# Early v loads issued from GpSimd's queue, and a new order of steps, in an attention and wave-mixing kernel

## The chip, the cores and the metric

The kernel runs on one core of a Trainium2 chip. A core has a matmul engine (TensorE, PE in the profile; its weight loads are PEld), a vector engine (VectorE, DVE), an activation engine (ScalarE, ACT), GpSimd (POOL) and SyncE (SP), which here only issues DMAs. Each engine works through its own queue in order and waits on semaphores for the others. Sixteen DMA engines move the data of all queues. The metric is the device time of one execution in microseconds; lower is better.

## The reference

Inputs are q, k and v of shape 8 batches x 8 heads x 576 positions x 64, and four weights. Everything is float32 outside the kernel; the kernel computes on bfloat16 tiles with float32 sums.

```python
q_d, k_d, v_d = (t.reshape(B, H, S // 4, 4, D).mean(axis=3) for t in (q, k, v))
out_up = np.repeat(sm_attn(q_d, k_d, v_d), 4, axis=2)       # pooled attention, repeated
mask = np.abs(pos[:, None] - pos[None, :]) < 4
out_local = softmax(where(mask, q @ k.T / 8, -1e9)) @ v     # a band of 7 positions
x = (out_up + out_local) with heads joined: (B, 576, 512)
theta = x @ w_theta
y = einsum(w_tok_r, x * cos(theta)) + einsum(w_tok_i, x * sin(theta))   # over positions
u = x + y
return u + maximum(u @ w_ch, 0)
```

## The kernel before, in words

A batch goes through these stages. Its inputs come in 13 loads into staging tiles `st` (15 buffers used in rotation, shared with the weights' loads): four k chunks and four q chunks of two heads each (288 KB), and five v chunks `v0` to `v4` of two windows of 64 positions each. A v chunk is loaded as two halves of 128 KB, one per window, with all eight heads; the half's rows are 64 positions x 8 heads of 256 bytes, so 512 runs. All loads are issued by SP (L220 for v, L223 for k and q, L253 and L255 for weights). Each chunk is then cast to bfloat16 (step C) on DVE, ACT or POOL.

PE turns k and q (A, L300), a copy takes the result out of PSUM (a), DVE and POOL form the sums of four positions (d, L317; e, L334 and L335 on POOL). The local attention has scores, exp, mask, outputs and their scaling (S, s, m, O, o, i). The pooled attention first sums v over four positions with a matmul against pooling matrices `pu` (U: L348 for the chunks 0 to 3, L350 for chunk 4), copies that out (u), spreads the last part with two products on POOL (x, L363), then has scores, exp, output and scaling (P, p, N, n). Both are joined in `xT` (T, t). Theta, its cosine and sine and the products with x follow (H, h, X, y), then the mix over positions (J, L654, against `WT`, which PE builds early from the token weights by the steps V and v), the sum with x (j, L663), the channel product (K, L693) and the last step with its store (b, D).

Constants (step k) are built on POOL: the identity `ident`, the `band`, three pooling matrices `pu`, and `own`; some fills are on DVE.

The order of all of this is written out by hand as one long string, `ORDER` (L66): each letter is the next step of its sequence, and the order of the letters is the order of the instructions on every engine's queue. `BANKS` (L81) gives the PSUM bank of each step that needs one, in that order, and `ENGINES` (L87) says for the steps C, a, c, f, q, u and v which engine does each copy (v DVE, a ACT, p POOL).

Of the kernel before, what the change touches and what calls it, by code (L numbers as in the profile page):

```python
# [26 lines left out]
W = 64  # L27
# [11 lines left out]

BY_QUEUE = [6, 7]  # L40

OC = 96


@with_exitstack
def kernel(
# [11 lines left out]
    nc = tc.nc  # L58
# [5 lines left out]


    ORDER = (  # L66
        "kLCLkLkCk2ACLCkaAkLCkLLCLLLCdlCaAAaaSkLkklSLLedSLLePsLCmsCOOmLkLsPpCCLlCookipULOuuxxLoCCOCNiioCCcN1l"
        "nLinTAAnnQcaClcaATLCmqtacCtOAHdTaoiSlhLXLdtyTeleLLsSPtsHPlCCmOpcLpSCsmloCTiOCcUlOtocuXuHoiOhcCiVhxom"
        "xNyiCGccHLALLganLVvVnLZVvLzNVlvVlXClvvLCnVnyCAQlvValhCACCveVLqXcvTtTcaAvlTtyaOoticHdTS2STsLsdecJHcJV"
        "LhcXttJvVhyVCVCvvvlXVyvLGVCVLVLgJLvZCvLVvvPjjjpCmJUjLuuHOxjoCiCOPJpxomiLNCXnHjLJnChNjAcLCJnyhCnLXjyT"  # L70
        "azCQLAAJCqaAlTLlLdJtLaSaLCjtOsoOiceJjjoCSLmLCJcTiClOtjsLCSCUHCRJeCuoiTTudRsCxLLjACtLJhaLtALJaGjmgOOj"
        "xPoJRoCiHiCcSpPjedCCXRKsLpmbyhKNZACnXbLHyaCLHhnXKyCLNhLLAbXzfKLCamUnSnyCuLfOJojCLiQRuCJJbAdsCLjJTmqR"
        "SjaOtjJCoseTAixxCatPPjpRLKdRDALLKJbCpSmbCOasToiNLtADnJLLjCnaNLLOnSHoiTLCjCJLnTtsOLjhotRCOCCLHXTiQohG"
        "HygDXiHThLmqhLCXZytztAKyTCabHODhLOteoLUumHDoiuiXRKhyRCfOCSbSJTsRoiLJsLdjCxADajtJejLPOpPLmopJxTDdtXjN"
        "JnnyDRjGJXCgNjHJmhniACHnaCCKjZLyLLCCbXQAChTdqRCKXyabKJySb2sLUjuKOzeutLSoesmCbCLCLSiJTmDJDjsCOPCjRpPo"
        "iJRLpOtjOoOoixHLioxTCChJiNAatnDJCHjDRndNALTLhKTtHnabnCtXeKQOjJyCoRbjGiTXgKhLHqKAFmhfLRZbJXbajyXAzJCy"
        "TyjtOaSJsoTiDtECjOromSUJuetTiKSRDsDstdOHjJJbHuxojTjJmthRiDPOYMOjhxJpJofiOomjiMOFjPoJpNiMjRNDnHnnofTn"
        "KKQbDhiGqEKTKbMtgHZRbyrzTKRhDTtYTyytbyHttKHDFJEGJhMjgbHjJDHhJMMjJrJZbMhDjyyjJzhDjRjyJjyKJJRJRKJYbJjD"
        "RKJjRjbjfRbJjDJjKjKjKKKfDREKbbRKDDbFDbbbrDDDYbD"
    )  # L80
    BANKS = (  # L81
        "0246024602467406240652064102456042605201650216452014601246012540160254602367012045106450164067340626"
        "4502610542612046025045620154062706420654205672065476025764205645074206742074620634062047016420176451"
        "0462107426107642076425062450215420346534203675204670246230463046230461346023026743126317430143064132"
        "604524360467253640234602043201450346751047236054176370101054231067542350167"
    )
    ENGINES = dict(  # L87
        C=(
            "vapaaaaavpvvappppppapppvpapppppppppppppvapvpappvappapppppppavpvapappaapppaaaaapppppaaaapapppappp"
            "appaavaa"  # L90
        ),
        a="avaavaaaavaaaaaaaaaaaaaaaaaaaaaa",
        c="aapapppappppppppappp",
        f="ppvpapap",
        q="vaaavvva",
        u="vavvavavaaaaaaaa",
        v="vvvvaaaavvvvaavaaa",
    )


# [25 lines left out]
    def copy(step, **operands):  # L126
        copies[next(engines[step])](**operands)  # L127
# [79 lines left out]
    def stage(key):  # L207
        t = staged[key] = rot("st", [P, S], FP32, 15)
        return t
# [3 lines left out]
    def load(b):  # L213
        for it in ITEMS:
            c = int(it[1])
            if it[0] == "v":
                t = stage((b, it))[:, 0:DM].rearrange("p (h d) -> p h d", d=D)
                for g in range(2):
                    lo = W0[2 * c + g]
                    nc.sync.dma_start(out=t[W * g:W * g + W], in_=v[b, :, lo:lo + W, :].rearrange("h p d -> p h d"))  # L220
            else:
                src = k if it[0] == "k" else q
                nc.sync.dma_start(out=stage((b, it)), in_=src[b, 2 * c:2 * c + 2].rearrange("h (p r) d -> (h p) (r d)", r=WR))  # L223
            yield
# [24 lines left out]
    def weight_loads():  # L249
        for kind, i, ct in WITEMS:  # L250
            t = stage((kind, i, ct))
            if kind == "tok":
                nc.sync.dma_start(out=t[0:OC], in_=(moe_w_tok_r, moe_w_tok_i)[i][OC * ct:OC * ct + OC, :])  # L253
            else:
# [3 lines left out]
    def weight_casts():  # L258
        for kind, i, ct in WITEMS:
            t = staged.pop((kind, i, ct))  # L260
            if kind == "tok":
                copy("c", out=w_tm[i][0:OC, ct, :], in_=t[0:OC])
            else:
# [5 lines left out]
    def weight_turns():  # L269
        for hf in range(2):  # L270
            for j in range(9):
                ps = held["w", hf, j] = one(BF16)
                for ct in range(3):
                    for ri in ((j % 2,) if j < 8 else (0, 1)):
                        lo, n = (0, P) if j < 8 else (HALF * ri, HALF)
                        nc.tensor.transpose(
                            out=ps[lo:lo + n, OC * ct:OC * ct + OC],
                            in_=w_tm[ri][0:OC, 3 * hf + ct, P * (j // 2):P * (j // 2) + n],
                            identity=ident[0:OC, 0:OC],
                        )  # L280
# [462 lines left out]
    def each(steps, n=B):  # L743
# [3 lines left out]
    sequences = {  # L747
        "k": constants(), "1": table(AF.Sin), "2": table(AF.Exp),
        "L": each(load), "C": each(cast), "l": weight_loads(), "c": weight_casts(), "V": weight_turns(), "v": weight_turns_out(),
        "A": each(turns), "a": each(turns_out), "d": each(key_sums), "e": each(query_sums),  # L750
        "U": each(pooled_v), "u": each(pooled_v_out), "x": each(pooled_v_last),
# [49 lines left out]
```

## Time and profile before

| | us |
|---|---|
| median of 3 runs | 246.65 |
| lowest, highest | 245.88, 248.42 |
| the profiled execution | 245.89 |
| its span, first to last instruction | 244.2 |
| mean granted TensorE clock | 0.979 |

The next lines are the page's list of DMA issues: what is loaded or stored, the engine that issues it, how many, the size of each, and the median time from issue to landing.

```profile
st<-in_v_dram SPq DMA_DIRECT2D x80, 128.0 KB, 5.1
st<-in_k_dram SPq DMA_DIRECT2D x32, 288.0 KB, 4.8
st<-in_q_dram SPq DMA_DIRECT2D x32, 288.0 KB, 5.3
out_dram<-osb SPq DMA_DIRECT2D x31, 256.0 KB, 3.3
```

All times are those of one execution. A row of a group gives the line, the engine, the operation, the tiles written and read with their shapes, the count, then busy time and the mean of one, and last the idle time of the engine just before them with what ended it. In the 40 slices each digit is the busy share of a slice in tenths. The chain is the work that ended last, followed back from the last instruction.

### The profile page before, as it was taken

To read this page: it belongs to the slowest core of one execution; us is meant where nothing else is said; L and a number is where in the kernel's file an instruction comes from. 1 tells how busy PE (TensorE), PEld (TensorE's weight loads), DVE (VectorE), ACT (ScalarE), POOL (GpSimd) and SP (SyncE) were. 2 spreads that over 40 slices of the span, in tenths; PEclk is the share of its full clock that TensorE was granted. 3 is DMA by queue.
4 is the path that set the end of the run, shared out by engine and by line. 5 is a ranking of instruction groups with operands and counts; after the bars stand their busy time and mean duration, and the time that the engine had idled before them with its cause. 6 is when DMAs were issued, how large, how long until landed. Compare 5 with 4: busy or idle time off the path is not lost.

```text
span 244.2 us, 8224 instructions
## 1 busy us (share of the span) xinstructions
PE 214.8 (88%) x3344; PEld 151.8 (62%) x3344; DVE 191.3 (78%) x393; ACT 164.9 (68%) x240; POOL 95.0 (39%) x170
## 2 busy tenths in 40 slices
PE   1466586998999999799999999999999999999990
PEld 1354453776678685487775786676676765667740
DVE  3596977797789879779799988897798978585453
ACT  3786497699799899798899859866677653420000
POOL 1785585776574594272056115923021000000000
PEclk9999997799999999999999999999999999999997
DMA  6999989989999999999899989997531586966577
GB/s 203 280 211 295 278 179 241 312 206 189 263 299 227 280 273 149 194 267 268 194 244 271 146 240 262 283 217 161 99 124 51 136 124 159 173 170 154 59 230 229
DMA packets 87671, 50.91 MB, mean 208 GB/s; under 512 B 72529, under 2 KB 72785, under 8 KB 87633
## 3 DMA queue, kind: packets, MB, share of 16 engines
q1 hardware_dynamic: 87632, 50.38, 91.7%
q8 instruction: 26, 0.43, 0.8%
q14 instruction: 13, 0.10, 0.2%
HBM read 34.11 MB, written 9.44 MB: 178 GB/s over the span
## 4 chain that ended last, share of the span: by engine, by line
PE 47%; DMA 22%; DVE 13%; SPq 7%; POOL 3%; issue 3%; ACT 3%; DVEq 0%; ACTq 0%; POOLq 0%
PE space L654 18%; DMA st<-in_v_dram 10%; PE space L567 7%; PE space L693 6%; DMA st<-in_q_dram 5%; SPq L220 4%; PE space L300 3%; DVE osb L706 2%; PE space L500 2%; DMA st<-in_moe_w_tok_i_dram 2%; PE space L540 2%; SPq L255 2%; DVE z L634 2%; DMA ur<-uT 1%; SPq L628 1%
## 5 line engine op out<-in xcount | busy, mean ns | idle before, releaser
L654 PE MATMUL space<-WT,z 128*128 128x288 bf16 x576 | 79.4, 286 | 0.8 <-DVE uT L663 0.4
L654 PEld LDWEIGHTS <-z 128*128 128x128 bf16 x576 | 54.0, 98 | 17.1 <-issue 1.3
L663 DVE TENSOR_TENSOR uT<-space,xT 128x288 bf16<-128x288 f32 x64 | 28.1, 449 | 11.5 <-PE space L654 9.6
L567 PE MATMUL space<-wth,xT 128*128 128x512 bf16 x128 | 33.8, 389 | 0.1
L693 PE MATMUL space<-wch,uT 128*128 128x512 bf16 (+1 forms) x132 | 31.9, 373 | 0.0
L706 DVE SCALAR_TENSOR_TENSOR osb<-space,ur 128x512 f32<-128x512 f32 (+1 forms) x33 | 21.7, 666 | 10.1 <-DMA ur<-uT 6.4
L574 ACT ACTIVATE cs<-space,pihc 128x512 bf16<-128x512 f32 x32 | 22.2, 693 | 7.9 <-issue 3.9
L520 DVE TENSOR_TENSOR tmp<-space,rl 128x512 bf16<-128x512 f32 x40 | 26.7, 679 | 0.5
L552 DVE TENSOR_TENSOR xT<-space,xdT 128x464 bf16<-128x464 f32 (+1 forms) x40 | 24.7, 627 | 1.7 <-PE space L540 1.4
L317 DVE TENSOR_REDUCE kd<-kT 128x290 bf16<-128x1160 bf16 x16 | 21.6, 1353 | 2.8 <-ACT kT L127 2.8
L480 ACT ACTIVATE pm<-space 128x1024 bf16<-128x1024 f32 (+1 forms) x24 | 20.6, 882 | 3.6 <-PE space L468 3.4
L334 POOL TENSOR_TENSOR two<-qT 128x576 f32<-128x576 bf16 x14 | 16.2, 1157 | 15.6 <-ACT qT L127 8.6
L127 POOL CAST q_tm<-st 128x576 bf16<-128x576 f32 x23 | 15.6, 685 | 15.6 <-DMA st<-in_q_dram 15.2
L127 POOL CAST k_tm<-st 128x576 bf16<-128x576 f32 x20 | 13.9, 700 | 18.8 <-DMA st<-in_k_dram 17.7
L127 POOL COPY ut<-uT 128x256 bf16<-128x256 bf16 x5 | 2.3, 451 | 44.5 <-DVE uT L663 44.5
L127 POOL CAST v_w<-st 128x512 bf16<-128x512 f32 x16 | 10.0, 634 | 23.9 <-DMA st<-in_v_dram 21.8
L575 ACT ACTIVATE cs<-space 128x512 bf16<-128x512 f32 x32 | 19.1, 598 | 0.0
L127 ACT COPY qT<-space 128x1152 bf16<-128x1152 bf16 x14 | 15.7, 1120 | 4.8 <-PE space L300 4.7
L693 PEld LDWEIGHTS <-uT 128*128 128x128 bf16 x132 | 12.1, 98 | 10.6 <-issue 0.3
L127 ACT COPY kT<-space 128x1152 bf16<-128x1152 bf16 x15 | 17.0, 1132 | 2.3 <-PE space L300 1.9
L567 PEld LDWEIGHTS <-xT 128*128 128x128 bf16 x128 | 11.5, 100 | 10.2 <-issue 0.8
L300 PE MATMUL space<-ident,k_tm 128*128 128x128 bf16 x144 | 12.1, 236 | 6.4 <-ACT k_tm L127 6.1
(95 smaller groups left out, 397.1 us busy)
## 6 DMA issues: line engine op xcount, KB each, us to landing
st<-in_v_dram SPq DMA_DIRECT2D x80, 128.0 KB, 5.1
st<-in_k_dram SPq DMA_DIRECT2D x32, 288.0 KB, 4.8
st<-in_q_dram SPq DMA_DIRECT2D x32, 288.0 KB, 5.3
out_dram<-osb SPq DMA_DIRECT2D x31, 256.0 KB, 3.3
st<-in_moe_w_tok_r_dram SPq DMA_DIRECT2D x6, 216.0 KB, 5.1
st<-in_moe_w_tok_i_dram SPq DMA_DIRECT2D x6, 216.0 KB, 4.8
out_dram<-osb SPq DMA_DIRECT2D x10, 128.0 KB, 2.5
st<-in_moe_w_theta_dram SPq DMA_DIRECT2D x4, 256.0 KB, 6.3
```

The source lines that it names most:

```text
L127: copies[next(engines[step])](**operands)
L300: nc.tensor.transpose(out=ps[:, P * r:P * r + P], in_=(k_tm if what == "k" else q_tm)[:, i, r, :, :], identity=ident)
L317: nc.vector.tensor_reduce(out=kd[:, hs, :, 0:PG].rearrange("p e g m -> p (e g) m"), axis=AX.X, op=ALU.add, in_=kT[:, hs, :].rearrange("p e ...
L480: nc.scalar.activation(out=pm.rearrange("p e c j w -> p e (c j w)"), in_=held.pop(("S", b, u))[:, :, 0:4 * W * n], func=AF.Exp, scale=SCL)
L520: nc.vector.tensor_tensor(out=tmp.rearrange("p g (j d) -> p g j d", d=D), in0=held.pop(("loc", b, c))[:, :, :, 0:D], in1=rls.pop((b, c)).u ...
L552: nc.vector.tensor_tensor(out=xT[:, :, CH * c:CH * c + cnt].rearrange("p e (m j) -> p e m j", j=4), in0=held.pop(("xT", b, c))[:, :, 0:cnt ...
L567: nc.tensor.matmul(out=th, lhsT=xT[:, dc, P * c:P * c + P], rhs=wth[:, dc, :], start=(dc == 0), stop=(dc == 3))
L574: nc.scalar.activation(out=cs[:, 0, :], in_=th, func=AF.Sin, bias=pihc, scale=1.0)
L654: nc.tensor.matmul(out=ps, lhsT=z[:, j, P * dc:P * dc + P], rhs=WT[:, j, 288 * hf:288 * hf + 288], start=(j == 0), stop=(j == 8))
L663: nc.vector.tensor_tensor(out=uT[:, dc, cols], in0=held.pop(("u", b, dc, hf)), in1=xT[:, dc, cols], op=ALU.add)
L693: nc.tensor.matmul(out=ps, lhsT=uT[:, dc, P * c:P * c + P], rhs=wch[:, dc, cols], start=(dc == 0), stop=(dc == 3))
L706: nc.vector.scalar_tensor_tensor(out=osb, in0=ps, scalar=0.0, in1=rest, op0=ALU.max, op1=ALU.add)
```

## The change

The two halves of each v chunk of the batches 0, 1 and 2 are issued by GpSimd in place of SP: 30 DMAs. The other 50 v loads, and all k, q and weight loads, stay with SP. Along with it come a new order, new banks and new engines for some copies. The numbers of steps stay the same, but for the steps 1 and 2, which load an activation table ahead of its use: four before, one after.

```diff
+EARLY = [0, 1, 2]
...
     ORDER = (
-        "kLCLkLkCk2ACLCkaAkLCkLLCLLLCdlCaAAaaSkLkklSLLedSLLePsLCmsCOOmLkLsPpCCLlCookipULOuuxxLoCCOCNiioCCcN1l"
-        "nLinTAAnnQcaClcaATLCmqtacCtOAHdTaoiSlhLXLdtyTeleLLsSPtsHPlCCmOpcLpSCsmloCTiOCcUlOtocuXuHoiOhcCiVhxom"
+        "LkCLkCL2kLLLCLkkLLAakCkACCLLCakACACaaLdLkSLLLCkLCSkeCSsCLeLdssULLlLlllmPOPuppOCmuCoOilOokixoCCCxiLNA"
+        "LonAnCLaNmaCiAdlTllnCnLCaAcaLTelcclCOTdoQeSqTCisctCLSTsttLtPCLLHmtPOocppLUOimuHLOoHcLLuchoxhilcxlich"
...
     ENGINES = dict(
...
-        a="avaavaaaavaaaaaaaaaaaaaaaaaaaaaa",
-        c="aapapppappppppppappp",
-        f="ppvpapap",
-        q="vaaavvva",
-        u="vavvavavaaaaaaaa",
-        v="vvvvaaaavvvvaavaaa",
+        a="avaaaaaaaaaavaaaavaaaaaavaaavaaa",
+        c="aapappvpvpppappppppa",
+        f="paaaaavp",
+        q="vvaaaaaa",
+        u="avvavvaaavavavvv",
+        v="vvvvvavvvvvvvvaaaa",
...
-                    nc.sync.dma_start(out=t[W * g:W * g + W], in_=v[b, :, lo:lo + W, :].rearrange("h p d -> p h d"))
+                    queue = nc.gpsimd if b in EARLY else nc.sync
+                    queue.dma_start(out=t[W * g:W * g + W], in_=v[b, :, lo:lo + W, :].rearrange("h p d -> p h d"))
```

Read out for POOL, the new order begins as follows (v chunks are two DMAs each, b0 is batch 0): ident; loads of b0 v0, v1, v2; band; loads of b0 v3, v4; the three `pu`; load of b1 v0; own; the two products L363 of b0; loads of b1 v1, v2, v3; cast of b1 q3; load of b1 v4; query sum, cast of th2, query sum of b1; casts of b1 v3 and v4 and of tok0.0, tok0.1; load of b2 v0; L363, cast of tok1.0, L363 of b1; load of b2 v1; casts of tok1.2, b2 k0, k1, q0; load of b2 v2; casts of b2 k2, k3, q2; loads of b2 v3, v4; then casts of the later token weights and of b2's v. Before, POOL's order was ident, cast of b0 q0, band, two `pu`, cast of b0 v1, the third `pu`, own, L363 of b0, six casts of b1's k and q, and so on.

On PE the new order has batch 0's turns (four), scores (three) and then the pooled sum U, ahead of its pooled scores P and outputs O; before, U stood behind both P steps and two O steps. The first mix of batch 0 (J) is step 347 of the string; it was step 295. Over the whole kernel the copies (C, c, a, f, q, u, v) on POOL go from 79 to 73, those on DVE from 33 to 42, those on ACT from 94 to 91.

## The prediction

> **What bounds the kernel now.** I read the page's shares and slices first, then the chain in order of time over the first 66 us, then the timelines of SP, POOL and PE there, and last the groups of POOL's operations. The first fence is the page: span, shares, slices, and the chain's line shares.
>
> ```profile
> span 244.2 us, 8224 instructions
> PE 214.8 (88%) x3344; PEld 151.8 (62%) x3344; DVE 191.3 (78%) x393; ACT 164.9 (68%) x240; POOL 95.0 (39%) x170
> PE   1466586998999999799999999999999999999990
> POOL 1785585776574594272056115923021000000000
> DMA  6999989989999999999899989997531586966577
> PE space L654 18%; DMA st<-in_v_dram 10%; PE space L567 7%; PE space L693 6%; DMA st<-in_q_dram 5%; SPq L220 4%; PE space L300 3%; DVE osb L706 2%; PE space L500 2%; DMA st<-in_moe_w_tok_i_dram 2%; PE space L540 2%; SPq L255 2%; DVE z L634 2%; DMA ur<-uT 1%; SPq L628 1%
> ```
>
> A slice is 6.1 us. From slice 8 on PE is nearly full; the first seven slices lack 3.4 of 7, so 21 of the 29 us in which PE does nothing lie before 43 us. Whatever moves that start moves the end almost one for one, since nothing after it has slack on PE. DMA is full from the second slice on. POOL has 39% in all, but 1, 7, 8, 5, 5, 8, 5, 5, 7, 6 tenths in the first ten slices: 35 us busy of 61. The next fence is the chain in order of time (start, us, what), where the start ends.
>
> ```profile
> 14.24 0.63 SPq L220
> 14.92 5.35 DMA st<-in_v_dram
> 20.35 0.62 ACT v_w L127
> ...
> 35.71 4.14 DMA st<-in_v_dram
> 39.91 0.62 ACT v_w L127
> ...
> 61.11 4.55 DMA st<-in_v_dram
> ```
>
> The last v chunk of each of the first three batches is the gate: its two halves are issued by SP, land some 5 us later, are cast, and PE's pooled sum goes on. Batch 0's cast ends at 20.97, batch 1's starts at 39.91; batch 2's last v half is issued by about 61.7.
>
> **What an issue costs.** The change takes 30 v issues (10 a batch) from SP and gives them to POOL, whose queue is in order, so POOL's compute waits behind each. These rows are SP's issues by tile (count, then min/median/max ns), and POOL's groups (busy us, mean ns).
>
> ```profile
> L220 SPq DMA_DIRECT2D st<-in_v_dram x80: 595/629/1716, 4.8 to 171.0; - x80
> L223 SPq DMA_DIRECT2D st<-in_k_dram x32: 332/422/1762, 0.8 to 152.4; - x32
> ```
>
> ```profile
> L334 POOL TENSOR_TENSOR two<-qT 128x576 f32<-128x576 bf16 x14 | 16.2, 1157 | 15.6 <-ACT qT L127 8.6 <-PE space L540 5.7 <-DVE qT L127 1.2
> L363 POOL TENSOR_TENSOR vd<-last,own 128x256 bf16<-128x256 bf16 x16 | 10.0, 639 | 10.4 <-ACT last L127 9.7 <-DVE last L127 0.7
> L335 POOL TENSOR_TENSOR qdT<-two 128x288 bf16<-128x288 f32 x14 | 9.4, 670 | 1.1
> ```
>
> On SP a v half (64 positions x 8 heads = 512 runs of 256 B) takes 595 ns at least, a k load (128 runs) 332: the issue grows with the runs. SP gains 30 x 0.63 = 18.9 us of queue time, about 6.3 per batch. No row shows what POOL pays, so call it x and bound it. Lower end 0.4 us, as a k issue on SP. For the upper end, treat a run as a step of a loop on POOL: L363 costs 639/256 = 2.5 ns an element, L335 2.3, L334 2.0. 512 x 2.5 = 1.28 us, and 0.1 for POOL's shortest instruction (the 128x1 memsets, 0.10) is 1.4; if reads and writes of a run are listed one after the other, 2.56 + 0.1 = 2.7 us. I take **1.4**, since POOL's own instructions are the nearer rows; 0.4 and 2.7 stay for the range.
>
> **The walk down POOL's queue.** Durations are from POOL's timeline. The new sequence is ident, v0 to v2 of batch 0 (6 issues), band, v3 and v4 (4 issues), then the three pooling matrices. ident ends at 1.37; band takes 1.84 (7.11 to 8.95), the matrices 2.51, 2.80 and 3.55. The last matrix is ready at 1.37 + 10.70 + 10x = **12.1 + 10x**. PE now has the pooled sum (L348, L350) right behind batch 0's turns and scores and ahead of its pooled scores and outputs, so all of these wait. Before, that sum ended on PE at 21.3 with two score and two output steps (about 1.5 us of PE) already done. Equal at x = 0.9; at 1.4 the matrix is there at 26.1, 5 us late, and the PE work pushed behind makes it 6.
>
> Batch 1: v0 (2x), own 0.82, the two products of L363 1.18, v1 to v3 (6x), one q cast 0.69, v4 (2x): the last issue ends at 14.8 + 20x, and with the 5.1 us to landing that DMA issues show for v, v4 is in at **19.9 + 20x**. Before: 39.9. Equal at x = 1.0; at 1.4, 47.9, **8.0 late**.
>
> Batch 2: up to its last v issue POOL has ident, band, matrices and own (1.37 + 11.52), two pairs of L363 (2.36), one pair of query sums (3.65), nine input casts (6.1) and five weight casts (3.3): 28.3 + 30x against 61.7. Equal at x = 1.1; at 1.4, 70.3, 8.6 late. The token weights' second half (tok0.3 on) is cast by POOL behind those issues, so the mix of batch 0 waits on the same queue.
>
> The three gates are not added: each carries the one before it. The last is the largest and I take it, **+8.6**.
>
> **What is taken off.** The loads that stay with SP (k, q, weights) go out earlier. It is hidden: the DMA row is full, so SP's lead becomes queue time in the engines, and the 15 staging buffers cap it, since a late v on POOL also holds its buffer and the loads behind it. Zero; if DMA had air in it, up to the 3.4 us of the cheap rival below. Casts moved off POOL in the new order are in the walk already (six copies fewer over the whole kernel, 3.8 us). DVE gets them: by the group rows its copies go from 17.7 to 24.0 us, +6.3, mostly v turns of weights, k and q casts and two turn copies; at 78% it has the room, except from 61 to 100 us (33.1 busy of 39), so I price it at 0 with 2 us if it shows. ACT: its functions alternate between exp and sin 22 times before and 16 times in the new order, and each table load is 1.283 us: 7.7 us off an engine that is not on the end's path; 0, at most 1 us gained. Banks: same 375 draws; 0. Work on PE is the same steps.
>
> Sum: 245.89 (the profiled execution, span 244.2) + 8.6 = 254.5; the median of the runs is 0.8 above that execution, so **255**.
>
> **Two rules against rows.** The Trainium skill, page "DMA: Bandwidth & Descriptors", section "Anatomy of one DMA", holds that descriptors are cheap in number on the GpSimd path, and its Specifications give about 1 us to the first byte; an estimate with x = 1.0 from that page would leave no gate more than 1.1 us later than today's and the time at about 247. This trace has no GpSimd DMA; the SP rows above (332 to 595 ns for four times the runs) speak for a cost by run.
>
> **Rivals.**
> Cheap issue, the other side (0.22). If x is near SP's 0.4 to 0.6, batch 0's v is issued by 3.2 + 10x = 7 to 9 us in place of 14.9, and DMA sets the pace: 8 x 0.295 + 10 x 0.131 = 3.67 MB at the windows' 250 GB/s, after 2.2 us, is 16.9 us against 20.3, 3.4 us sooner. By batch 1's last v some 9.3 MB must have passed, 39.3 us against 39.9, so part is given back; with ACT's 1 us I get 2 to 4.5 us: 242 to 244.5, say 243. For it: POOL is idle 26 of the first 61 us, and SP's issues stand in the chain (L220 4%). It decides where x is under 0.9. Against it: 512 runs an issue.
>
> No change (0.16). x is 0.9 to 1.1, or DMA caps any lead: 246 to 248. For it: the full DMA row. The same page, section "Issuing engines are not separate DMA queues", says a second issuing engine saves only the sequencer's time to issue; by that rule alone the sum would be near zero, and the DMA row agrees with it (9 tenths from slice 2).
>
> Dear issue (0.10). x of 2.2 or more: batch 1's v4 at 63.9 or later, 24 us late, of which most reaches the end: over 269.
>
> My forecast (0.52) is x from about 1.15 to 2.2: batch 1's gate 3 to 24 late, 249.5 to 269.
>
> **How the numbers follow.** 255 is the likeliest case. The range leaves out the dear case (0.10) and the better part of the cheap one (0.10): 242.5 to 269. Alone, the forecast case has 249.5 to 269. A difference under 1% (2.5 us) is about what a measurement of this kernel can tell from none. Faster 0.22 (the cheap case, whose figure of 243 is 1.5% below 246.65), within 1% 0.16, slower 0.62 (0.52 + 0.10).
>
> **What would show it.** POOL's timeline must show ten v issues between ident and the last pooling matrix, ending near 26 us, and PE idle before L348 until then. The first v_w cast of batch 1's v4 near 48. POOL's tenths in slices 1 to 12 go to 8 or 9, and the first full slice of PE moves one to two slices to the right. If POOL's issues are 0.6 us or less, step one is wrong and with it the sign. If they are long but PE's early slices are unchanged, the walk is wrong: POOL's queue then doesn't hold up what I said it holds. If v lands much later than 5 us after its issue, sharing between two queues in the DMA engines, which I priced at nothing, is the cause.

## The result, and the profile after

| | median, us | lowest to highest | runs |
|---|---|---|---|
| before | 246.26 | 245.65 to 248.42 | 4 |
| after | 253.61 | 252.77 to 255.04 | 4 |

The ratio is 1.0288, with a 95% interval of 1.0205 to 1.0371: slower by 7 us. The prediction said 255.0, in 242.5 to 269. The profiled execution took 253.0 us (span 251.3, mean granted clock 0.978; before 245.89, 244.2 and 0.979), so the mean clock does not explain the difference. The time came out as forecast, but not by the way that was forecast; that is what the rest is about.

The first lines are of the page of the changed kernel: span, engines, tenths in 40 slices (6.3 us each), DMA queues (packets, MB, share), the chain's shares by line, POOL's issues as a group (busy us, mean ns), and issues with their time to landing.

```profile
span 251.3 us, 8188 instructions
PE 214.1 (85%) x3321; PEld 152.4 (61%) x3344; DVE 197.2 (78%) x402; ACT 155.6 (62%) x228; POOL 109.9 (44%) x194
PE   1115876984999999999979999999999999999990
POOL 8872795997699455673651244030006100000000
DMA  6999999999999999998799589995657148577777
q1 hardware_dynamic: 71792, 46.45, 80.8%
q0 software_dynamic: 1440, 3.93, 8.0%
PE space L657 27%; PE space L570 10%; PE space L696 7%; DMA st<-in_q_dram 6%; PE space L303 4%; DMA st<-in_v_dram 3%; PE space L543 3%; PE space L503 2%; PE space L471 2%; PE space L622 2%; SPq L631 1%; POOL st L223 1%; PE space L417 1%; PE space L588 1%; DMA k_tm<-xT 1%
L223 POOL DMA_DIRECT2D st<-in_v_dram x30 | 20.7, 696 | 1.7 <-ACT q_tm L129 1.5
st<-in_q_dram SPq DMA_DIRECT2D x32, 288.0 KB, 6.1
st<-in_v_dram SPq DMA_DIRECT2D x50, 128.0 KB, 3.8
st<-in_v_dram POOLq DMA_DIRECT2D x30, 128.0 KB, 8.0
```

Four things stand there. An issue on POOL takes 0.69 us, not 1.4. PE's work is the same (214.1 us, 214.8 before), and the time lost is idle time on PE: 37.2 us of the span (251.3 less 214.1) in place of 29.4. Two holes are new in the PE row, slices 2 and 3 (1 and 1; 4 and 6 before) and slice 10 (4; 8 before). And the v loads that POOL issues land 8.0 us after their issue; the median of SP's 80 was 5.1.

The timelines of two engines come next (start, us for the group, engine, line, operation, and in brackets the idle time before it with what ended it). First POOL, up to the last pooling matrix:

```profile
1.51 4.23 POOL L223 DMA_DIRECT2D st<-in_v_dram  x6
...
7.47 2.71 POOL L223 DMA_DIRECT2D st<-in_v_dram  x4
...
17.78 0.47 POOL L159 COPY pu<-full 64x32 bf16<-64x32 bf16 x2
```

The last pooling matrix is ready at 18.25 us. PE's work does not wait for it: the pooled sum (L351) starts at 23.23, and what holds PE before that stands here:

```profile
5.14 1.14 PE L303 MATMUL space<-ident,k_tm 128*128 128x128 bf16 x9 [5.14 <-ACT k_tm L129]
10.86 1.12 PE L303 MATMUL space<-ident,q_tm 128*128 128x128 bf16 x9 [4.58 <-DVE vd L177]
13.49 1.12 PE L303 MATMUL space<-ident,k_tm 128*128 128x128 bf16 x9 [1.51 <-DVE k_tm L129]
19.55 1.14 PE L303 MATMUL space<-ident,q_tm 128*128 128x128 bf16 x9 [4.95 <-ACT q_tm L129]
...
23.23 0.62 PE L351 MATMUL space<-v_w,pu 128*32 128x512 bf16 x4
...
63.05 0.65 PE L543 MATMUL space<-ident,tmp 128*128 128x116 bf16 x5 [3.28 <-issue]
```

Batch 0's four turns start at 5.14, 10.86, 13.49 and 19.55; before they started at 5.18, 8.39, 10.46 and 11.88. The last line is the other hole: 3.28 us in which PE has no releaser that the profile knows ("issue"), in the middle of one line's matmuls. The chain of the changed kernel (start, us, what) names what the turns waited for:

```profile
4.10 14.71 DMA st<-in_q_dram
...
33.01 8.61 DMA st<-in_v_dram
...
59.77 3.28 issue
```

Batch 0's last q load is issued at 4.10 and lands at 18.8. No k or q load of batch 0 was moved; v loads of the same batch are now under way beside them.

How the two queues share the DMA engines is seen in the list of queues for the 2 us from 10 to 12 us (packets, MB, share of the engines' time):

```profile
DMA packets 186, 0.44 MB, mean 218 GB/s; under 512 B 38, under 2 KB 38, under 8 KB 186
q0 software_dynamic: 79, 0.22, 53.8%
q1 hardware_dynamic: 107, 0.22, 49.6%
```

q0 is POOL's queue, q1 SP's. In these 2 us each gets half of the bytes; over the whole time that the q load is under way, from 4.10 to 18.8 us, POOL's queue moves 1.31 of 3.58 MB, which is all of batch 0's v. In one queue, as before, the k and q loads that SP issued first went first; in two queues the v loads that are needed later take their share from them.

### The profile page after: what moved, and what is told of

It is laid out like the page before. It is cut to its first block, busy times and chain, and to the rows that moved or that the text cites. A ratio compares the mean times of both kernels' runs of the same rounds, so it can differ in the third digit from the quotient of the medians.

```text
span 251.3 us, 8188 instructions
## 1 busy us (share of the span) xinstructions
PE 214.1 (85%) x3321; PEld 152.4 (61%) x3344; DVE 197.2 (78%) x402; ACT 155.6 (62%) x228; POOL 109.9 (44%) x194
## 3 DMA queue, kind: packets, MB, share of 16 engines
q0 software_dynamic: 1440, 3.93, 8.0%
## 4 chain that ended last, share of the span: by engine, by line
PE 65%; DMA 13%; DVE 8%; issue 5%; SPq 3%; POOL 2%; ACT 2%; DVEq 0%; POOLq 0%; ACTq 0%
PE space L657 27%; PE space L570 10%; PE space L696 7%; DMA st<-in_q_dram 6%; PE space L303 4%; DMA st<-in_v_dram 3%; PE space L543 3%; PE space L503 2%; PE space L471 2%; PE space L622 2%; SPq L631 1%; POOL st L223 1%; PE space L417 1%; PE space L588 1%; DMA k_tm<-xT 1%
## 5 line engine op out<-in xcount | busy, mean ns | idle before, releaser
L657 PE MATMUL space<-WT,z 128*128 128x288 bf16 x576 | 77.9, 286 | 0.0
L570 PE MATMUL space<-wth,xT 128*128 128x512 bf16 x115 | 33.3, 399 | 1.0 <-issue 0.4
L129 POOL CAST v_w<-st 128x512 bf16<-128x512 f32 x23 | 14.8, 648 | 40.4 <-DMA st<-in_v_dram 29.0
L696 PE MATMUL space<-wch,uT 128*128 128x512 bf16 (+1 forms) x123 | 31.0, 372 | 0.6 <-issue 0.2
L555 DVE TENSOR_TENSOR xT<-space,xdT 128x464 bf16<-128x464 f32 (+1 forms) x40 | 24.1, 623 | 4.3 <-PE space L543 4.2
L223 POOL DMA_DIRECT2D st<-in_v_dram x30 | 20.7, 696 | 1.7 <-ACT q_tm L129 1.5
L303 PE MATMUL space<-ident,q_tm 128*128 128x128 bf16 x144 | 12.1, 236 | 10.0 <-ACT q_tm L129 5.3
L129 POOL COPY ut<-uT 128x256 bf16<-128x256 bf16 x2 | 0.8, 396 | 42.1 <-DVE uT L666 42.1
L570 PEld LDWEIGHTS <-xT 128*128 128x128 bf16 x128 | 11.9, 102 | 11.6 <-issue 1.9
L129 POOL CAST q_tm<-st 128x576 bf16<-128x576 f32 x17 | 11.4, 679 | 16.4 <-DMA st<-in_q_dram 16.4
L543 PE MATMUL space<-ident,tmp 128*128 128x116 bf16 (+1 forms) x160 | 14.6, 217 | 4.1 <-issue 3.3
```

The lines of the kernel that those rows point to most:

```text
L223: queue.dma_start(out=t[W * g:W * g + W], in_=v[b, :, lo:lo + W, :].rearrange("h p d -> p h d"))
L303: nc.tensor.transpose(out=ps[:, P * r:P * r + P], in_=(k_tm if what == "k" else q_tm)[:, i, r, :, :], identity=ident)
L543: nc.tensor.matmul(out=ps[:, kk::2, STEP * g:STEP * g + OWN[n]], lhsT=tmp[:, g, P * kk:P * kk + P], rhs=identw[:, :, lo:lo + OWN[n]], star ...
L555: nc.vector.tensor_tensor(out=xT[:, :, CH * c:CH * c + cnt].rearrange("p e (m j) -> p e m j", j=4), in0=held.pop(("xT", b, c))[:, :, 0:cnt ...
L570: nc.tensor.matmul(out=th, lhsT=xT[:, dc, P * c:P * c + P], rhs=wth[:, dc, :], start=(dc == 0), stop=(dc == 3))
L657: nc.tensor.matmul(out=ps, lhsT=z[:, j, P * dc:P * dc + P], rhs=WT[:, j, 288 * hf:288 * hf + 288], start=(j == 0), stop=(j == 8))
```

## The experiments

Each is compared with the kernel before on the same chip. All kernels but the second have the new order; line numbers are those of the changed kernel.

**One part each.** In the first, only the order, banks and engines are new, and SP issues all v loads. In the second only the queue is new, and the old strings stand.

```diff
-EARLY = [0, 1, 2]
+EARLY = []
```

> The new order, banks and engines of copies, but all v loads stay on SP, behind batch 0's q loads. Crowding theory (v of batch 0, sent from POOL's queue at 1.5 us, takes DMA time from batch 0's k and q, so that PE starts late): the third group of turns on PE is back near 10.5 us and the fourth near 12 (13.5 and 19.6 with the change), time 245 to 248. Occupancy theory (30 issues of 0.69 us = 20.7 us on POOL hold its casts and matrices back): also 245 to 248. Order theory (the new order itself costs the 7 us): 252 to 254.

```diff
     ORDER = (
-        "LkCLkCL2kLLLCLkkLLAakCkACCLLCakACACaaLdLkSLLLCkLCSkeCSsCLeLdssULLlLlllmPOPuppOCmuCoOilOokixoCCCxiLNA"
+        "kLCLkLkCk2ACLCkaAkLCkLLCLLLCdlCaAAaaSkLkklSLLedSLLePsLCmsCOOmLkLsPpCCLlCookipULOuuxxLoCCOCNiioCCcN1l"
...
```

> The old order, banks and engines, with the 30 v loads of batches 0 to 2 on POOL. Crowding theory: in the old order batch 0's v0 and v1 stand behind the constants' first step and the first POOL cast, which waits for q0, so that v starts some 5 us later than in the change; part of k and q has landed by then: 248 to 252. Occupancy theory: POOL has more casts in the old order, so it is worse than the change: 255 to 260. Order theory: 245 to 248.

Measured: the order alone 249.55 us, ratio 1.0127 (1.0081 to 1.0174); the queue alone 264.32 us, 1.0728 (1.0663 to 1.0792). Neither came out as a theory had it: the order alone lies between the ranges 245 to 248 and 252 to 254, the queue alone above the highest, 255 to 260.

The order alone costs 3 us, and PE's turns start as before. Its largest wait on PE between 24 and 55 us is this (PE's timeline):

```profile
31.48 0.46 PE L471 MATMUL space<-qT,kT 64*64 64x64 bf16 x32 [0.91 <-ACT qT L129]
35.50 0.55 PE L543 MATMUL space<-ident,tmp 128*128 128x116 bf16 x4 [3.57 <-DVE xdT L129]
```

That `xdT` stands in DVE's queue behind a cast of v before which DVE sat idle for 4.78 us, until 32.83, for one of batch 1's v loads. The kernel's chain runs through the next of these loads, from 28.27 on, which lands 5.56 us later. The largest wait there before was 2.6 us.

In the queue alone, POOL's issues do come late, as the prediction feared. The page's slices and POOL's timeline:

```profile
POOL 1988599683696528852712540195202100000000
...
DMA  7999299802999949969999696999774247756876
```

```profile
18.94 0.47 POOL L159 COPY pu<-full 64x32 bf16<-64x32 bf16 x2
19.35 2.71 POOL L223 DMA_DIRECT2D st<-in_v_dram  x4
...
24.72 0.47 POOL L159 COPY pu<-full 64x32 bf16<-64x32 bf16 x2
...
57.12 1.38 POOL L223 DMA_DIRECT2D st<-in_v_dram  x2
```

In the old order the v issues stand behind casts that wait for their own inputs. Batch 0's last four v loads go out at 19.35 (before from 12.92 on), batch 2's first two at 57.12, the third pooling matrix is ready at 25.2, and the DMA row falls to 2, 0 and 2 tenths. In the first of these slices SP waits 4.7 us for a staging buffer that a cast of k on POOL frees; in the other two its queue stands behind one transposing DMA (L612) that waits 12.6 us for DVE's `zT`. On the chain there, two mask products of DVE (L491) take 3.5 and 4.3 us, where the same products take about 0.7 and 0.5 at the median; why, no run here tells, so not all of the 7.3% is shown to be POOL's queue. The new order makes the new queue bearable, and the two must not be judged apart. An issue costs 0.68 us here too.

**Which batch on which queue.** Only the list of early batches is changed: first batches 1 and 2, then each batch by itself.

```diff
-EARLY = [0, 1, 2]
+EARLY = [1, 2]
```

> The change, with batch 0's v back on SP; batches 1 and 2 stay on POOL (20 issues, 13.8 us of POOL). Crowding theory: the start is free again, so 5 to 7 us of the 7 come back: 246 to 249. Occupancy theory: two thirds of the loss stay: 250 to 252. Order theory: 252 to 254.

```diff
-EARLY = [0, 1, 2]
+EARLY = [0]
```

> The change for batch 0 alone (10 issues, 6.9 us of POOL, all in the first 10.2 us); batches 1 and 2 back on SP. Crowding theory: the start is as late as with the change, PE's fourth group of turns near 19.5 us: 251 to 254. Occupancy theory: one third of the loss: 248 to 249.5. Order theory: 252 to 254.

```diff
-EARLY = [0, 1, 2]
+EARLY = [1]
```

> New order, with batch 1's ten v loads alone on POOL; batches 0 and 2 on SP. Theory (PE stops for 3 to 5 us near 60 us because its own next instructions are fetched late while batch 2's v loads of POOL's queue are under way): those loads are on SP's queue again here, so no such stop, start as before the change (PE's four turns by about 12 us), and the time that of the new order alone, 249.5 to 250.5, ratio 1.012 to 1.017. Rival (any v load on POOL in a full DMA stage costs by the share it takes from SP): batch 1 costs half of what batches 1 and 2 cost together, 251 to 252, with the loss before 45 us.

```diff
-EARLY = [0, 1, 2]
+EARLY = [2]
```

> New order, with batch 2's ten v loads alone on POOL; batches 0 and 1 on SP. Theory (late fetch of PE's instructions under POOL's loads of batch 2): the stop near 60 us is there, 3 to 5 us long, with no releaser, and the time is 252 to 253.5, ratio 1.023 to 1.03, as with batches 1 and 2 together. Rival (share by batch): 251 to 252, spread over 45 to 75 us, no single stop of over 2 us.

The changed kernel was also run once more beside the last two, unedited:

> The changed kernel once more, beside the two above. Its ratio should be 1.025 to 1.035 again. If the stop near 60 us belongs to the program and not to one execution, the profile has it again, 2.5 to 4.5 us long, in the second half of PE's turns of batch 2; if it was an accident of one execution, PE's idle time between 55 and 66 us is under 1.5 us.

Measured, with the time in which PE is not busy by stretch (length of the stretch less PE's busy time in it, from the windows of each profile; the sum is the span less PE's busy time on the page):

```
                     median us  ratio (95%)              PE not busy, us, in the stretch
                                                      0-24  24-55  55-66  66-end   sum
before               246.26  -                        12.3    6.8    1.2    9.1   29.4
order alone          249.55  1.0127 (1.0081-1.0174)   12.2    8.8    1.5   10.9   33.4
batch 0 on POOL      250.68  1.0186 (1.0125-1.0246)   17.8    5.9    0.8   10.5   35.0
batch 1 on POOL      249.21  1.0144 (1.0090-1.0198)   13.7    7.4    0.9   11.1   33.1
batch 2 on POOL      251.43  1.0221 (1.0158-1.0284)   12.3   10.7    3.4    9.3   35.7
batches 1, 2         253.20  1.0255 (1.0187-1.0322)   14.0    6.5    5.2    7.8   33.5
all three            253.61  1.0288 (1.0205-1.0371)   17.5    6.2    3.9    9.7   37.2
all three, again     254.82  1.0378 (1.0305-1.0450)   17.9    8.2    4.3    8.4   38.9
```

Over the order alone, batch 0 adds 0.6%, batch 1 adds 0.2% and batch 2 adds 0.9%: 1.7% in sum, and 1.6% (2.5% in the second series) for all three together. With intervals of half a per cent and more each, the step for all three is clear of noise, and what one batch adds is not. The crowding theory missed both of its ranges, 246 to 249 for batches 1 and 2 (253.20 measured) and 251 to 254 for batch 0 (250.68): the start is worth less than it held, the later batches more. Batch 1 came out as expected, batch 2 a little cheaper than the 1.023 to 1.03 given for it, and the changed kernel's second ratio a little over its 1.025 to 1.035. The profile with batches 1 and 2 has a clock of 0.965 and 217.7 us of PE work, so its sum of idle time says less than its ratio; the profile with batch 2 alone is of its longest execution (254.61), so only its stop is read here.

If batch 0's v crowds its k and q, the late start has to be there whenever that v is on POOL, and only then. It is: 17.5 to 17.9 us of PE idle by 24 us with it, 12.2 to 14.0 without. But most of it is caught up in the next stretch in the kernel with batch 0 alone (5.9 us against 8.8), so 5.6 us at the start are worth some 1.5 at the end (250.68 less 249.55 is 1.1; the ratios differ by 0.6%), which is not clear of noise.

The second hole belongs to batch 2. PE's waits between 55 and 66 us, first with batch 1 alone, then PE's timeline with batch 2 alone:

```profile
PE space L657 <- DMA z<-zT: 0.5, 1, 0.5
```

```profile
60.17 0.32 PE L543 MATMUL space<-ident,tmp 128*128 128x116 bf16 x3
63.44 0.65 PE L543 MATMUL space<-ident,tmp 128*128 128x116 bf16 x5 [2.95 <-issue]
```

With batch 1 alone no wait there is over 0.5 us; with batch 2 alone PE stops for 2.95 us in the same place as the changed kernel, after the third of the eight transposes of one L543 group. The repeat of the changed kernel has it again (3.6 us), so it is the program's and not one execution's.

What PE waits for is in the trace's records of the instruction queue (q8): PE's instructions come in pieces of 16 KB, some 128 weight loads each. The same piece, in every kernel of the new order (the last four are described below):

```
                     piece fetched     PE weight loads   PE stops, after   runs again,
                     us to us          begun by then     733 weight loads  after the piece
order alone          55.84 - 57.11          704              1.18 us          1.55 us
batch 0 on POOL      56.78 - 58.22          647              none
batch 1 on POOL      55.16 - 56.34          683              none
batch 2 on POOL      60.64 - 61.97          733              3.21 us          1.46 us
batches 1, 2         60.88 - 62.24          733              4.89 us          1.47 us
all three            60.31 - 61.64          733              3.54 us          1.40 us
all three, again     62.09 - 63.40          733              3.90 us          1.38 us
all, v later         62.61 - 63.93          730              2.75 us          1.55 us
products on POOL     55.65 - 57.29          690              1.69 us          1.64 us
batches 1, 2 by ACT  60.91 - 61.99          600              none
batch 0 by ACT       63.80 - 64.73          624              none
```

(The times of this table are between starts of weight loads.) Wherever PE stops, it is behind the same instruction, and it runs again 1.4 to 1.6 us after the piece has landed. In all five profiles with batch 2's v on POOL the fetch starts only when PE has run out or all but (730 to 733 begun); in the six others it starts at 600 to 704. PE is not faster there: it goes through the 128 weight loads before the stop in 5.5 us in the order alone and in the changed kernel alike, and the fetch starts 3.8 us after the first of them in the one, 6.3 us in the other. The queues of the changed kernel from 60 to 62 us:

```profile
q0 software_dynamic: 108, 0.32, 82.5%
q1 hardware_dynamic: 111, 0.14, 28.5%
q8 instruction: 1, 0.02, 4.2%
```

In those 2 us POOL's queue, with batch 2's last v loads, holds the engines for most of the time. That the stop is a late fetch is shown; that the fetch is late because it stands in line behind POOL's packets is argued from this window and from the table, since no record tells when the piece was asked for. A stop of this kind is not POOL's alone: with every load on SP, the order alone has one of 1.18 us and the kernel with products on POOL one of 1.69 us.

PE is slow behind the stop, too. In the changed kernel the granted clock is 0.50 from 63.0 to 66.4 us; four matmuls of L570 take 1.91 us there and 1.03 us at 67.25. From 55 to 72 us the mean granted clock is 0.80 to 0.90 in all five profiles with batch 2's v on POOL, and 1.00 in the kernel before, the order alone, batch 0, batch 1 and the products. An estimate from these figures: 3.4 us at half clock cost 1.7 us of PE, which no column of idle time counts. Why the clock falls there no run tells.

**POOL's time alone.** Is it POOL's occupied queue that hurts? The next kernel has all loads on SP and puts on POOL, in the place of each of the 30 issues, a product of 128x256 elements.

```diff
-                    queue = nc.gpsimd if b in EARLY else nc.sync
-                    queue.dma_start(out=t[W * g:W * g + W], in_=v[b, :, lo:lo + W, :].rearrange("h p d -> p h d"))
+                    if b in EARLY:
+                        wide = ident.unsqueeze(1).to_broadcast([P, 2, P])
+                        nc.gpsimd.tensor_tensor(out=idle, in0=wide, in1=wide, op=ALU.mult)
+                    nc.sync.dma_start(out=t[W * g:W * g + W], in_=v[b, :, lo:lo + W, :].rearrange("h p d -> p h d"))
```

> All v loads on SP in the new order (249.55 as measured without POOL work), and in the place of each of the 30 POOL issues a product of 128x256 elements on POOL whose result nobody reads: 30 x 0.64 = 19.2 us of POOL's queue, as the issues' 20.7, without their DMAs. Occupancy theory: POOL's queue is what the v issues cost, so the time is near the change's: 252.5 to 254.5. DMA theory (it is where and when the packets run, not POOL's time): 249 to 250.5.

Measured: 250.19 us, ratio 1.0183 (1.0080 to 1.0285), with PE idle for 11.9 us by 24 us, much as with the order alone (12.2), and 1.4 us from 55 to 66 (1.5). The products take POOL 19.6 us in all. The interval overlaps those of the order alone and of the changed kernel, so the time by itself does not decide, and some cost of POOL's occupancy, 0.6% over the order alone by the ratios, is neither shown nor ruled out. But neither hole of the changed kernel is there, so these two are not POOL's occupied queue.

**Batch 0's v later on POOL.** If v crowds k and q at the start, issue it later: the band and two pooling matrices go ahead of the v loads on POOL.

```diff
-        "LkCLkCL2kLLLCLkkLLAakCkACCLLCakACACaaLdLkSLLLCkLCSkeCSsCLeLdssULLlLlllmPOPuppOCmuCoOilOokixoCCCxiLNA"
+        "LkCLkCL2kLLLCLkkLkkkkkLAaCACCLLCaACACaaLdLSLLLCLCSkeCSsCLeLdssULLlLlllmPOPuppOCmuCoOilOokixoCCCxiLNA"
```

> The change, with band and the first two pooling matrices ahead of batch 0's ten v issues on POOL instead of between and behind them: the same work on POOL, the last matrix at the same time, but v starts near 8.5 us instead of 1.5, behind most of batch 0's k and q. Crowding at the start: PE's fourth group of turns goes from 19.6 us to 12 to 14, PE's idle time up to 24 us from 17.5 to 14 or less, time 251 to 252.5 (what batches 1 and 2 cost stays). Occupancy theory: nothing changes, 253 to 254.5.

Measured: 253.15 us, ratio 1.0297 (1.0199 to 1.0395), no better than the changed kernel, where 251 to 252.5 was expected of crowding. The turns are mended: PE's four begin at 5.07, 8.07, 9.55 and 10.87, so the crowding was their cause. PE's idle time by 24 us stays at 16.9 us (14 or less expected). What came instead is in ACT's timeline:

```profile
9.38 1.43 ACT L129 CAST q_tm<-st 128x576 bf16<-128x576 f32 x2 [0.69 <-DMA st<-in_q_dram]
17.06 0.62 ACT L129 CAST v_w<-st 128x512 bf16<-128x512 f32 x1 [6.25 <-DMA st<-in_v_dram]
17.59 1.11 ACT L129 COPY kT<-space 128x1152 bf16<-128x1152 bf16 x1
```

ACT's queue has a cast of batch 0's v ahead of the copies of `kT` and `qT`. That v now shares the engines with batch 1's k and q, which SP has issued meanwhile, and comes 6.25 us late for ACT; PE waits 7.51 us for `qT`. The loss moved by one load and stayed as large.

**Another second queue.** If two queues as such are the trouble, a queue that issues as SP's does should show it too. ACT issues the v loads of batches 1 and 2, or of batch 0.

```diff
-EARLY = [0, 1, 2]
+EARLY = [1, 2]        # the seventh;  [0] the eighth
...
-                    queue = nc.gpsimd if b in EARLY else nc.sync
+                    queue = nc.scalar if b in EARLY else nc.sync
```

> As the run with batches 1 and 2 alone off SP (253.2), but their 20 v DMAs are issued by ACT instead of POOL: again a second queue beside SP's, but packets of 256 bytes instead of 4096. If it is POOL's large packets that make PE's instruction loads late: the stall of 3 to 5 us on PE near 59 us (in the middle of the transposes, no releaser) is 1.3 us or less, time 249 to 251.5, the rest being ACT's 20 x 0.6 = 12 us. If any second queue does it: the stall stays and the time is 252 to 255.

> As the run with batch 0 alone off SP (250.7), but its ten v DMAs are issued by ACT, in packets of 256 bytes beside SP's of 2304. If the size of the packets sets the share of the two queues: k and q keep nearly all of it, PE's fourth group of turns is at 12 to 15 us (19.5 with POOL), time 249 to 251, less ACT's own 6 us where they are in the way. If two queues share in equal time: the fourth group stays at 18 to 20 us and the time at 250 to 253.

Measured: 262.9 us, ratio 1.0742 (1.0667 to 1.0818), and 257.29 us, 1.0490 (1.0410 to 1.0570). Both are far above their ranges and slower than the same loads on POOL (1.0255 and 1.0186), for a reason of their own, seen in ACT's timeline of the kernel with batch 0 (ACTq is what ACT issues):

```profile
9.44 8.07 ACTq L223 DMA_DIRECT2D st<-in_v_dram  x4
17.55 1.25 ACT L129 CAST q_tm<-st 128x576 bf16<-128x576 f32 x2 [7.96 <-DMA st<-in_v_dram]
```

Four issues hold ACT for 8.07 us, and its casts of q stand behind them; PE's fourth turns start at 18.85. With batches 1 and 2 the same happens from 28.0 us on (four issues, 3.82 us; the cast behind them had ACT idle for 7.46 us). PE does not stop for its instructions near 60 us in either (table above), as the expectation for POOL's large packets had it, but with batches 1 and 2 on ACT PE had lost 13.2 us between 24 and 55 us to other waits and the fetch had that much more time. So these two runs don't tell whether a second queue of SP's kind would be harmless; they show that ACT, with casts behind its issues, is a bad issuer while the DMA engines are full.

No version here is faster than the kernel before.

## Why the prediction was right in its number and wrong in its way

**The bound: right.** PE's idle time grew by 7.8 us (29.4 to 37.2) at 0.7 us less of work. Of that, 5.2 lie before 24 us and 2.7 between 55 and 66; from 24 to 55 it is 0.6 less, and all that follows adds 0.6. So the idle time that was added lies in the first 66 us. (POOL had less room before than the prediction says: it read the eighth slice as 5 tenths where the row has 7, and by the windows of that profile POOL was busy for 39.4 of 61 us, not 35. The sum does not use it.)

**The issue cost: the step that failed.** "I take 1.4, since POOL's own instructions are the nearer rows": 30 issues took 20.7 us, 682 ns at the median and 851 at most, within the bounds but half of the value taken. An issue is no loop over 512 runs at an element's price; SP's 629 ns for the same load was the nearer row. The page "DMA: Bandwidth & Descriptors" of the Trainium skill, section "Anatomy of one DMA", which was set aside, holds that descriptors are cheap in number; 512 runs for 682 ns agree with it.

**The walk: right in form, and against the forecast.** With 0.69 it puts the last pooling matrix at 19.0 (18.25 measured), before any use of it. Batch 1's v4 would be in at 33.7 and batch 2's last v issued at 49.0, both earlier than before; by the walk the kernel is faster, and the cheap rival (243 us) is the case whose condition came true. Measured, batch 1's v4 is in at 41.6 (33.01 and 8.61 in the chain), and batch 2's last v issue ends at 56.8 (61.7 before). The issues are earlier than before, by less than the walk says, since it counted POOL's own work and not its waits for inputs; batch 1's v is late all the same, because it takes 8.6 us and not 5.1 to land.

**SP's lead and the sharing of the engines: priced at nothing, and the first cause.** The prediction held that a full DMA row would hide any lead, and named late landings as what would show sharing. They came: 8.0 us at the median, and 14.7 us for the q load that gates the start. The row was as full as before; what changed is who is served first. The Trainium skill, same page, section "Queues, rings and completion order", says that a DMA engine takes turns between the queues it has work for, a packet at a time. That both queues moved data in the same 2 us, 0.22 MB each, agrees with it; turns one for one the records do not show, 54 packets of 4096 B from POOL beside 96 of 2304 B from SP. The rule that the prediction named beside its case of no change ("Issuing engines are not separate DMA queues": a second issuer saves only issue time) gave the wrong sum: bytes and engine time were indeed unchanged, the order of landing was not. With batch 0 alone on POOL the late start is worth some 0.6% at the end, within the noise.

**PE's instructions: not in the prediction at all.** The stop of 3 to 5 us near 60 us, with batch 2's v on POOL, was in no term and no rival, and neither was the lower clock behind it. Batch 2 alone adds 0.9% to the order, at the edge of the noise.

**Order and banks at zero: wrong.** They cost 1.27% alone, 3 us, although six of the 22 table loads are gone, as priced (ACT 164.9 to 155.6 us busy) and DVE's extra copies are there (191.3 to 197.2). Which of the moved steps it is was followed only to the 3.57 us wait behind batch 1's v; the rest stays open.

So +8.6 was forecast from a queue on POOL that holds PE up, which the traces of the changed kernel do not show, and +7 came from three things that were priced at nothing or not at all. That the two sums lie so close is luck. Late issues on POOL, as forecast, are seen with the queue alone in the old order (+7.3% in all), where they stand behind casts that wait; the new order had put that right.

## What to carry to other kernels

Loads that are moved to a second queue no longer wait their turn: while the DMA engines are full they take a share from the loads that are needed first. Before moving some, list what lands late in the stretch in which both queues are busy, and price that, not the issue. An order and a queue that were made together are to be measured together, and a time that comes out as forecast is no proof of the reason.

## What the runs showed of the hardware

- An issue of 512 runs of 256 B takes POOL 0.69 us, beside 0.63 on SP. In the trace's records the 3.93 MB of POOL's queue go in 960 packets of 4096 B (and 480 of 4 B), where SP moves v in packets of 256 B; a packet of 4096 B takes an engine about 0.3 us and one of 256 B about 0.018, so 16 runs cost the same either way.
- Two busy queues got equal halves of the bytes from 10 to 12 us, 0.22 MB each; from 4.10 to 18.8 us POOL's queue got 1.31 of 3.58 MB.
- PE stopped for 1.2 to 4.9 us with no semaphore involved, because a 16 KB piece of its own instructions came late while the DMA engines were full. It ran again 1.4 to 1.6 us after the piece had landed. The Trainium skill, page "Advanced Engine Details and Errata", section "ISA Cache", gives an instruction cache lines of 16 KB, 256 instructions each; the pieces here have that size.
- Issues on ACT held that engine for up to 8 us while the DMA engines were full (four loads); on POOL no issue of the changed kernel took over 0.851 us.
